# One moving part of 512 slots for the first products of the second mixture of experts

## The chip, the cores and the metric

The kernel runs on one core of a Trainium2 chip. The metric is device time in microseconds (us) of one execution, the median of several; lower is better. TensorE is called PE in the profile, VectorE DVE, ScalarE ACT, GpSimd POOL, and SyncE's DMA queue SP.

## What is computed

The reference chains linear attention, a dense two-layer network and a mixture of experts. The part that is changed is the last:

```python
for e in range(E):                      # 8 experts
    for k in range(2):                  # a token's first and second choice
        mask = top2[:, k] == e
        h = np.maximum(x[mask] @ w1[e], 0.0)        # [tokens, 512] @ [512, 1024]
        out[mask] += top2_w[mask, k, None] * (h @ w2[e])   # [tokens, 1024] @ [1024, 512]
```

There are 2304 tokens of 512 values; each goes to two of eight experts, so an expert has about 576 of them.

## The kernel before

Each expert has room for 640 slots (`CAP`), five blocks of 128 (`NB`); the first four are the early ones (`EARLY` = 512). All arithmetic of the experts is in pairs of fp32r numbers: a value is kept as a high part and the rest, and `mm3` (L170) makes one product out of three matmuls: high by high (L173), high by low (L174) and low by high (L175).

For an expert `e` these steps exist. `gather(e, j)` (L862) fetches a block of 128 token rows with indirect DMAs on POOL: one DMA of whole rows for experts 0 and 1 (L871), four DMAs of quarter rows for experts 2 to 7 (L866). `gtrans(e, j)` (L875) turns the block (on PE for experts 0 and 1, on DVE for the others) and splits it into `xgT[e]`, contraction on the partitions. `load_w1`, `load_w2` fetch the weights through SP, and `split_w1`, `split_w2` split them on ACT and DVE. `h2_step(e, f)` (L888) makes one of eight blocks of 128 hidden units: the stationary operand is a 128 by 128 block of `s1`, the moving one `xgT[e]` over the slots, the contraction has four parts, so with `mm3` there are twelve matmuls for each moving part. The result is then taken out of PSUM on ACT (relu, high part, L902) and DVE (low part, L903) into `hT`. `y2_step(e, j)` (L908) makes the second product for one block of slots, 24 matmuls of 512 columns with `hT` stationary, scales it on ACT, and adds it to the output with an indirect DMA on POOL (L917).

The moving part of `h2_step` is at most 512 columns, so 640 slots go in two: 384 and 256 (`HALVES`), both in one PSUM tile of two banks from the pool `py`, which has two such tiles. Step f+2 therefore needs step f to be out of PSUM. For expert 0 the first 512 slots are made early, during the last routing work (`PARTS[:1]`), and the last 128 later (`PARTS[1:]`, eight steps of twelve matmuls of 128 columns), between the second products of its blocks 2 and 3.

The order of all instructions is written out by hand (`tc.manual_schedule`): each engine runs its instructions in the order of the program, and semaphores are set from the tiles' dependencies. In the loop over experts from 1 on (L1095), the gathers and `load_w1` of the next expert come first in program order, then eight `h2_step`s of this expert with `split_w2` after every second, then `load_w2` of the next expert, then five `y2_step`s with the next expert's `split_w1` and `gtrans` between them.

Of the kernel before, what the change touches and what calls it, by code (L numbers as in the profile page):

```python
# [7 lines left out]
F32 = mybir.dt.float32  # L8
F32R = mybir.dt.float32r
# [3 lines left out]
AF = mybir.ActivationFunctionType  # L13
ALU = mybir.AluOpType
# [24 lines left out]
def attn_moe_moe2_kernel(  # L39
# [14 lines left out]
    nc = tc.nc  # L54
    B, H, S, D = q.shape
    NT = B * S
    DM = H * D
    DFF = w_in.shape[1]
    E, _, F2 = w1.shape
    P = 128  # L60
# [3 lines left out]
    NPR = DM // P  # L64
# [3 lines left out]
    NF2 = F2 // P  # L68
    CAP = 640
    NB = CAP // P  # L70
    EB = 4
    EARLY = EB * P
    PARTS = [(0, EARLY), (EARLY, CAP - EARLY)]
    HALVES = [(0, 384), (384, CAP - 384)]
    NE = 2
    NOB = (NT - CAP + P - 1) // P
    LSTRIDE = CAP + NOB * P
# [24 lines left out]
    ident = cst.tile([P, P], F32, name="ident")  # L102
# [32 lines left out]
    py = work.enter_context(tc.tile_pool(name="py", bufs=2, space=PSUM))  # L135
    pa = work.enter_context(tc.tile_pool(name="pa", bufs=2, space=PSUM))
# [5 lines left out]
    def SS(shape, dt, name):  # L142
        return sp.tile(shape, dt, tag="S", name=name)

    def XX(shape, dt, name):
        return xp.tile(shape, dt, tag="X", name=name)

    def HH(shape, dt, name):
        return hp.tile(shape, dt, tag="H", name=name)
# [4 lines left out]
    def TT(shape, dt, name):  # L154
        return tp.tile(shape, dt, tag="T", name=name)

    def MM(shape, name):
        return pm.tile(shape, F32, tag="M", name=name)

    def split_lo(lo, src, hi, eng=None):  # L160
        (eng or nc.vector).tensor_tensor(out=lo, in0=src, in1=hi.bitcast(F32), op=ALU.subtract)  # L161

    def split(alloc, src, shape, name, eng=None):
        hi = alloc(shape, F32R, name + "h")
        lo = alloc(shape, F32R, name + "l")
        nc.scalar.copy(hi, src)
        split_lo(lo, src, hi, eng)
        return hi, lo

    def mm3(out_ap, stat, mov, ssl, msl, start, stop):  # L170
        sh, sl = stat
        mh, ml = mov
        nc.tensor.matmul(out_ap, sh[ssl], mh[msl], start=start, stop=False)  # L173
        nc.tensor.matmul(out_ap, sh[ssl], ml[msl], start=False, stop=False)  # L174
        nc.tensor.matmul(out_ap, sl[ssl], mh[msl], start=False, stop=stop)  # L175
# [8 lines left out]
    def quarters_transposed(t, name):  # L184
        u = TT([P, NPR, P], F32, name)
        nc.vector.transpose(out=u.rearrange("p c (g a) -> p g c a", a=Q), in_=t.rearrange("p g (c b) -> p g c b", b=Q))
        return u
# [626 lines left out]
    raw1, raw2, s1, s2, xg, xgT, hT = {}, {}, {}, {}, {}, {}, {}  # L814

    def load_w1(e, i):
        raw1[e, i] = (HH if e == 0 else SS)([P, F2], F32, f"w1_{e}_{i}")
        nc.sync.dma_start(out=raw1[e, i], in_=quads(w1[e], i) if e >= NE else w1[e, i * P:(i + 1) * P, :])

    def load_w2(e, i):  # L820
        raw2[e, i] = SS([P, 2, DM], F32, f"w2_{e}_{i}")
        nc.sync.dma_start(out=raw2[e, i], in_=w2[e, 2 * i * P:2 * (i + 1) * P, :].rearrange("(a p) c -> p a c", p=P))

    def split_w1(e, i):
        s1[e, i] = split(W, raw1[e, i], [P, F2], f"s1_{e}_{i}")

    def split_w2(e, i):
        s2[e, i] = split(W, raw2[e, i], [P, 2, DM], f"s2_{e}_{i}", nc.gpsimd if e == 0 and i < 2 else None)
# [46 lines left out]
    def gtrans(e, j):  # L875
        if j == 0:
            xgT[e] = (XX([P, NPR, CAP], F32R, f"xgh{e}"), XX([P, NPR, CAP], F32R, f"xgl{e}"))
        if e >= NE:
            t = quarters_transposed(xg[e, j], f"xgt{e}_{j}")
        else:  # L880
            t = MM([P, NPR, P], f"xgp{e}_{j}")
            for c in range(NPR):
                nc.tensor.transpose(t[:, c, :], xg[e, j][:, c * P:(c + 1) * P], ident)
        hi, lo = (u[:, :, j * P:(j + 1) * P] for u in xgT[e])
        nc.scalar.copy(hi, t)
        split_lo(lo, t, hi)

    def h2_step(e, f, parts=HALVES):  # L888
        if len(parts) == 2:
            ps = py.tile([P, 2, DM], F32, tag="Y", name=f"h2_{e}_{f}")  # L890
            banks = [ps[:, i, :] for i in range(2)]
        else:
            banks = [pa.tile([P, DM], F32, tag="A", name=f"h2_{e}_{f}_{parts[0][0]}")]
        for (a, n), bk in zip(parts, banks):
            for c in range(NPR):
                mm3(bk[:, :n], s1[e, c], xgT[e], (slice(None), slice(f * P, (f + 1) * P)),
                    (slice(None), c, slice(a, a + n)), c == 0, c == NPR - 1)
        if (e, f // 2) not in hT:
            hT[e, f // 2] = (HH([P, 2, CAP], F32R, f"hTh{e}_{f}"), HH([P, 2, CAP], F32R, f"hTl{e}_{f}"))
        for (a, n), bk in zip(parts, banks):  # L900
            hi, lo = (t[:, f % 2, a:a + n] for t in hT[e, f // 2])
            nc.scalar.activation(hi, bk[:, :n], AF.Relu)  # L902
            nc.vector.scalar_tensor_tensor(out=lo, in0=bk[:, :n], scalar=0.0, in1=hi.bitcast(F32),  # L903
                                           op0=ALU.max, op1=ALU.subtract)

    adds = {}

    def y2_step(e, j, between={}):  # L908
        ps = pa.tile([P, DM], F32, tag="A", name=f"y2_{e}_{j}")
        for f in range(NF2):  # L910
            mm3(ps, tuple(t[:, f % 2] for t in hT[e, f // 2]), s2[e, f // 2], (slice(None), slice(j * P, (j + 1) * P)), (slice(None), f % 2),
                f == 0, f == NF2 - 1)
            if f in between:
                between[f]()
        t = TT([P, DM], F32, f"y2s{e}_{j}")
        nc.scalar.activation(t, ps, AF.Copy, scale=lst[:, e, j, 1:2].bitcast(F32))  # L916
        i = nc.gpsimd.indirect_dma_start(out=out, out_offset=bass.IndirectOffsetOnAxis(ap=lst[:, e, j, 0:1], axis=0),  # L917
                                         in_=t, in_offset=None, compute_op=ALU.add)
        nc.gpsimd.memset(spacer, 0)


        for o in adds.get(e, []):
            tc.declare_no_dep(i.ins, o.ins, reason="a token has one slot of an expert")
        for o in adds.get(e - 1, []):
            tc.add_manual_dep(i.ins, o.ins.name, mybir.DependencyInfo(mybir.DependencyClass.Sync, mybir.DependencyReason.DATA),
                              reason="adds to the same rows")
        adds.setdefault(e, []).append(i)


    with tc.manual_schedule():  # L930
# [64 lines left out]
        for g in range(NG):  # L995
# [42 lines left out]
            for f in range(NF):  # L1038
                ps = h_step(g, f)
# [32 lines left out]
            load_w1(1, i)  # L1072
        rus = route_units(NG - 1)
        for f in range(NF2):
            h2_step(0, f, PARTS[:1])
            for x in PLAN["r5"].split():
                if int(x.split("@")[1]) == f:
                    rus[x.split("@")[0]]()
            if f % 2:
                split_w2(0, f // 2)  # L1080
# [8 lines left out]
        for j in range(EB, NB):  # L1089
            gather(0, j)  # L1090
            gather(1, j)
        y2_step(0, 0)
        y2_step(0, 1)
        y2_step(0, 2, {4: lambda: gtrans(0, 4)})
        for e in range(E):  # L1095
            nx = e + 1 < E
            if nx and e:
                for j in range(NB):
                    gather(e + 1, j)
                for i in range(NPR):  # L1100
                    load_w1(e + 1, i)
            for f in range(NF2):
                h2_step(e, f, HALVES if e else PARTS[1:])
                if e and f % 2 == 0:
                    split_w2(e, f // 2)
                if e == 0 and f % 2:
                    gtrans(1, f // 2)
            if nx:
                for i in range(NF2 // 2):
                    load_w2(e + 1, i)  # L1110
            for j in range(NB):
                if e == 0 and j < EB - 1:
                    continue
                if nx:
                    if e:
                        if j < NPR:
                            split_w1(e + 1, j)
                        gtrans(e + 1, j)
                    elif j == EB - 1:
                        for i in range(NPR):  # L1120
                            split_w1(1, i)
                    else:
                        gtrans(1, j)
                y2_step(e, j)
    work.close()


    with ExitStack() as oc:
# [5 lines left out]
        with tc.If(most > CAP):  # L1134
            with tc.For_i(0, E, 1) as e:
# [7 lines left out]
                for m in range(NOB):  # L1143
# [3 lines left out]
                    pt = op.tile([P, NPR, P], F32, name="opt")  # L1147
# [12 lines left out]
                    for f in range(NF2):  # L1160
# [4 lines left out]
                        out=out, out_offset=bass.IndirectOffsetOnAxis(ap=ol[:, m, 0:1], axis=0),  # L1165
# [31 lines left out]
```

## Time and profile before

| | |
|---|---|
| median of three runs | 1051.83 us (1051.07 to 1052.28) |
| the profiled execution | 1058.36 us |
| its span, first to last instruction | 1056.7 us |
| PE busy | 968.6 us, 92% |
| experts 1 to 7, first to last product | 572.77 to 1043.34 us |
| mean granted TensorE clock | 0.952 of full |

The page tells busy time for each engine and, in 40 slices, where it falls. "Idle before, releaser" is the time an engine sat idle ahead of an instruction and what ended it. "issue" means that nothing shown released it, "remote" that a semaphore came in whose sender isn't known. The times of matmuls overlap, so what one costs in a stream is read from start to start, not from its own length.

### The profile page before, as it was taken

How to read it: one execution, taken by the hardware profiler on the slowest of the kernel's cores; microseconds unless marked ns; L12 is line 12 of the kernel's file. 1: busy time of each engine (PE TensorE's matmuls, PEld its weight loads, DVE VectorE, ACT ScalarE, POOL GpSimd, SP SyncE). 2: the span in 40 equal slices, each digit the busy share in tenths (PEclk: the TensorE clock that was granted, in tenths of full speed). 3: DMA queues.
4: the chain of work that ended last, by engine and by line, in shares of the span. 5: the costliest groups of instructions: out<-in, count | busy, mean ns of one | idle time of the engine just before them, and what ended most of it. 6: DMA issues, size and time to landing. Idle time of an engine off the chain costs nothing.

```text
span 1056.7 us, 12905 instructions
## 1 busy us (share of the span) xinstructions
PE 968.6 (92%) x4897; PEld 818.0 (77%) x4897; DVE 553.7 (52%) x978; ACT 427.1 (40%) x688; POOL 293.9 (28%) x342
## 2 busy tenths in 40 slices
PE   7989799999999999999999599697996997969994
PEld 7457578888888888898789499686886886868993
DVE  7899947964795567568434143242432523325320
ACT  3756544634463445467424132232331422314320
POOL 4002100150024003106342515427145162361111
PEclk8999899999999999999999799899898998989998
DMA  7688508600800120030652335244252442522203
GB/s 208 199 234 210 68 1 190 209 2 18 177 17 1 46 55 1 1 120 22 239 137 70 120 85 125 70 117 113 71 120 80 113 127 62 126 92 61 31 11 41
DMA packets 107282, 100.08 MB, mean 95 GB/s; under 512 B 58320, under 2 KB 82896, under 8 KB 107216
## 3 DMA queue, kind: packets, MB, share of 16 engines
q1 hardware_dynamic: 95664, 78.17, 26.2%
q0 software_dynamic: 11552, 21.04, 10.6%
q8 instruction: 40, 0.66, 0.3%
q14 instruction: 26, 0.21, 0.1%
HBM read 78.46 MB, written 20.72 MB: 94 GB/s over the span
## 4 chain that ended last, share of the span: by engine, by line
PE 74%; DVE 9%; issue 6%; another core or an unknown queue 5%; ACT 4%; DMA 1%; POOL 0%; DVEq 0%; POOLq 0%; SPq 0%; ACTq 0%
PE y L174 12%; PE y L173 12%; PE y L175 12%; PE h L175 11%; PE h L173 11%; PE h L174 10%; PE xp L495 2%; DVE stage L566 2%; ACT hTh L902 1%; PE kvp L381 1%; DVE hTl L903 1%; DVE stage L565 1%; PE qTp L482 1%; DVE hs L613 1%
## 5 line engine op out<-in xcount | busy, mean ns | idle before, releaser
L903 DVE SCALAR_TENSOR_TENSOR hTl<-h,hTh 128x384 fp32r<-128x384 f32 (+3 forms) x128 | 62.8, 491 | 233.7 <-ACT hTh L902 168.3
L902 ACT ACTIVATE hTh<-h 128x384 fp32r<-128x384 f32 (+3 forms) x128 | 56.0, 438 | 228.4 <-PE h L175 83.2
L917 POOL DMA_INDIRECT out_dram<-y2s,lst x40 | 63.3, 1581 | 282.9 <-ACT y2s L916 282.6
L866 POOL DMA_INDIRECT xg<-x2d,lq x120 | 118.9, 991 | 35.9 <-issue 33.1
L613 DVE SCALAR_TENSOR_TENSOR hs<-hs 128x512 f32<-128x512 f32 (+1 forms) x80 | 55.2, 690 | 54.5 <-ACT hs L612 52.7
L173 PE MATMUL h<-xgh,s_0h 128*128 128x384 f32 (+3 forms) x128 | 43.9, 343 | 43.1 <-DVE hTl L903 25.0
L438 POOL TENSOR_TENSOR q<-q,qm 128x1024 f32<-128x1024 f32 (+1 forms) x10 | 18.2, 1818 | 209.3 <-DVE qm L437 132.0
L612 ACT COPY hs<-h 128x512 f32<-128x512 f32 (+1 forms) x80 | 43.3, 541 | 76.7 <-PE h L175 73.1
L916 ACT ACTIVATE y2s<-y,lst 128x512 f32<-128x512 f32 x40 | 27.6, 689 | 91.3 <-PE y L175 76.4
L799 POOL DMA_INDIRECT lstd<-rrow,rsi x36 | 43.3, 1201 | 67.5 <-DVE rsi L796 61.6
L173 PEld LDWEIGHTS h<-xgh,s_0h 128*128 128x128 f32 x128 | 25.7, 201 | 46.9 <-DVE hTl L903 27.8
L624 ACT CAST g<-hs 128x512 fp32r<-128x512 f32 (+1 forms) x72 | 41.3, 573 | 37.8 <-DVE hs L613 37.7
L161 DVE TENSOR_TENSOR g<-hs,g 128x512 fp32r<-128x512 f32 (+1 forms) x72 | 44.9, 624 | 0.5 <-ACT g L624 0.5
L175 PE MATMUL h<-xgh,s_3l 128*128 128x384 f32 (+3 forms) x128 | 41.2, 322 | 2.9 <-issue 2.6
L175 PE MATMUL h<-xgh,s_0l 128*128 128x384 f32 (+3 forms) x128 | 41.9, 327 | 1.9 <-issue 1.9
L173 PE MATMUL h<-xgh,s_1h 128*128 128x384 f32 (+3 forms) x128 | 41.8, 327 | 1.7 <-issue 1.5
L174 PE MATMUL h<-xgl,s_0h 128*128 128x384 f32 (+3 forms) x128 | 42.1, 329 | 1.3 <-issue 1.3
L174 PE MATMUL h<-xgl,s_2h 128*128 128x384 f32 (+3 forms) x128 | 41.6, 325 | 1.1 <-issue 1.1
L173 PE MATMUL h<-xgh,s_2h 128*128 128x384 f32 (+3 forms) x128 | 41.4, 323 | 1.3 <-issue 1.3
L175 PE MATMUL h<-xgh,s_1l 128*128 128x384 f32 (+3 forms) x128 | 41.3, 323 | 1.3 <-issue 1.3
L174 PE MATMUL h<-xgl,s_1h 128*128 128x384 f32 (+3 forms) x128 | 41.5, 324 | 0.9 <-issue 0.8
L175 PE MATMUL h<-xgh,s_2l 128*128 128x384 f32 (+3 forms) x128 | 41.5, 324 | 0.6 <-issue 0.6
(341 smaller groups left out, 2914.4 us busy)
## 6 DMA issues: line engine op xcount, KB each, us to landing
w<-in_moe_w_dram SPq DMA_DIRECT2D x64, 512.0 KB
stage<-in_moe_w_in_dram SPq DMA_DIRECT2D x16, 512.0 KB
stage<-in_moe_w_out_dram SPq DMA_DIRECT2D x16, 512.0 KB
out_dram<-zero SPq DMA_DIRECT2D x1, 4864.0 KB
x2d<-x2s SPq DMA_DIRECT2D x9, 512.0 KB
k<-in_k_dram SPq DMA_DIRECT2D x12, 256.0 KB
v<-in_v_dram SPq DMA_DIRECT2D x12, 256.0 KB
x2q<-x2d SPq DMA_DIRECT2D x24, 128.0 KB
```

The source lines that it names most:

```text
L161: (eng or nc.vector).tensor_tensor(out=lo, in0=src, in1=hi.bitcast(F32), op=ALU.subtract)
L173: nc.tensor.matmul(out_ap, sh[ssl], mh[msl], start=start, stop=False)
L174: nc.tensor.matmul(out_ap, sh[ssl], ml[msl], start=False, stop=False)
L175: nc.tensor.matmul(out_ap, sl[ssl], mh[msl], start=False, stop=stop)
L612: nc.scalar.copy(hs, ps)
L613: nc.vector.scalar_tensor_tensor(out=hs, in0=hs, scalar=0.01, in1=hs, op0=ALU.mult, op1=ALU.max)
L624: nc.scalar.copy(parts[0], hs)
L799: i = nc.gpsimd.indirect_dma_start(out=lstd, out_offset=bass.IndirectOffsetOnAxis(ap=si[:, kk, r:r + 1], axis=0), in_=row[:, kk, r, :], in ...
L866: nc.gpsimd.indirect_dma_start(out=t[:, g, :], out_offset=None, in_=x2d.rearrange("n (i c) -> (n i) c", c=P), in_offset=bass.IndirectOffse ...
L902: nc.scalar.activation(hi, bk[:, :n], AF.Relu)
L903: nc.vector.scalar_tensor_tensor(out=lo, in0=bk[:, :n], scalar=0.0, in1=hi.bitcast(F32), op0=ALU.max, op1=ALU.subtract)
L917: i = nc.gpsimd.indirect_dma_start(out=out, out_offset=bass.IndirectOffsetOnAxis(ap=lst[:, e, j, 0:1], axis=0), in_=t, in_offset=None, com ...
```

## The change

`h2_step` now moves 512 slots in one part, into half a tile of `py`: steps f and f+1 share a tile, so two tiles hold four steps. The last 128 slots are made by a new function, `h2_late`: there the 128 slots are the stationary operand and the hidden units move, twice 512 columns, twelve matmuls each. The result has slots on the partitions; it goes through relu into two tiles of `TT` (one on ACT, one on DVE), and `turn`, called later, transposes it on PE in eight blocks of 128 by 128 into two tiles of `MM`, and splits it from there into the last 128 columns of `hT`. `turn` is called in the first `y2_step` of an expert after its sixth of eight blocks (for expert 0 in its fourth `y2_step`). All experts are treated so, expert 0 too. For expert 0 the `gtrans` of expert 1 and its `split_w1` are placed anew among the `y2_step`s, since the eight late steps that they lay between are gone.

```diff
-    HALVES = [(0, 384), (384, CAP - 384)]
-    def h2_step(e, f, parts=HALVES):
...
+    def h2_step(e, f):
+        n = EARLY
+        if f % 2 == 0:
+            h2p[e] = py.tile([P, 2, DM], F32, tag="Y", name=f"h2_{e}_{f}")
+            hT[e, f // 2] = (HH([P, 2, CAP], F32R, f"hTh{e}_{f}"), HH([P, 2, CAP], F32R, f"hTl{e}_{f}"))
+        ps = h2p[e][:, f % 2, 0:n]
+        for c in range(NPR):
+            mm3(ps, s1[e, c], xgT[e], (slice(None), slice(f * P, (f + 1) * P)),
+                (slice(None), c, slice(0, n)), c == 0, c == NPR - 1)
+        hi, lo = (t[:, f % 2, 0:n] for t in hT[e, f // 2])
+        nc.scalar.activation(hi, ps, AF.Relu)
+        nc.vector.scalar_tensor_tensor(out=lo, in0=ps, scalar=0.0, in1=hi.bitcast(F32),
+                                       op0=ALU.max, op1=ALU.subtract)
+
+    def h2_late(e):
+        a = EARLY
+        ps = py.tile([P, 2, DM], F32, tag="Y", name=f"h2l{e}")
+        for i in range(2):
+            for c in range(NPR):
+                mm3(ps[:, i, :], xgT[e], s1[e, c], (slice(None), c, slice(a, CAP)),
+                    (slice(None), slice(i * DM, (i + 1) * DM)), c == 0, c == NPR - 1)
+        t = [TT([P, DM], F32, f"h2l{e}_{i}") for i in range(2)]
+        nc.scalar.activation(t[0], ps[:, 0, :], AF.Relu)
+        nc.vector.tensor_scalar(out=t[1], in0=ps[:, 1, :], scalar1=0.0, scalar2=None, op0=ALU.max)
+
+        def turn():
+            for i in range(2):
+                pt = MM([P, NPR, P], f"h2lT{e}_{i}")
+                for c in range(NPR):
+                    nc.tensor.transpose(pt[:, c, :], t[i][:, c * P:(c + 1) * P], ident)
+                for j in range(NPR // 2):
+                    hi, lo = (u[:, :, a:CAP] for u in hT[e, i * NPR // 2 + j])
+                    nc.scalar.copy(hi, pt[:, 2 * j:2 * j + 2, :])
+                    split_lo(lo, pt[:, 2 * j:2 * j + 2, :], hi)
+        return turn
...
-        y2_step(0, 0)
-        y2_step(0, 1)
-        y2_step(0, 2, {4: lambda: gtrans(0, 4)})
-        for e in range(E):
+        y2_step(0, 0, {4: lambda: gtrans(1, 0)})
+        y2_step(0, 1, {4: lambda: gtrans(1, 1)})
+        y2_step(0, 2, {2: lambda: gtrans(0, 4), 5: lambda: gtrans(1, 2)})
+        turn = h2_late(0)
+        for i in range(NF2 // 2):
+            load_w2(1, i)
+        split_w1(1, 0)
+        split_w1(1, 1)
+        y2_step(0, 3, {5: turn})
+        split_w1(1, 2)
+        y2_step(0, 4, {1: lambda: gtrans(1, 3), 3: lambda: split_w1(1, 3), 5: lambda: gtrans(1, 4)})
+        for e in range(1, E):
...
             for f in range(NF2):
-                h2_step(e, f, HALVES if e else PARTS[1:])
-                if e and f % 2 == 0:
+                h2_step(e, f)
+                if f % 2 == 0:
                     split_w2(e, f // 2)
-                if e == 0 and f % 2:
-                    gtrans(1, f // 2)
+            turn = h2_late(e)
...
-                y2_step(e, j)
+                y2_step(e, j, {} if j else {5: turn})
```

## Rows read from the trace of the kernel before

**Rows 1.** The page, part 1: busy time, share of span, instructions.
```profile
PE 968.6 (92%) x4897; PEld 818.0 (77%) x4897; DVE 553.7 (52%) x978; ACT 427.1 (40%) x688; POOL 293.9 (28%) x342
```

**Rows 2.** First products by stretch (experts 1, 2, 6, 7): length, PE, PEld, DVE, ACT, clock, DMA.
```profile
572.77:618.64 45.87, 34.44 (x192) 32.45 (x191) 6.87 (x14) 6.05 (x14) 0.81 0.35 104
645.87:686.81 40.94, 31.73 (x192) 30.62 (x191) 6.87 (x14) 6.14 (x14) 0.87 0.32 86
...
919.57:960.60 41.03, 31.68 (x192) 30.23 (x191) 6.87 (x14) 6.14 (x14) 0.88 0.30 87
987.83:1015.95 28.12, 28.12 (x192) 28.08 (x191) 6.88 (x14) 6.14 (x14) 1.00 0.07 10
```

**Rows 3.** Timeline of ACT, experts 3 and 0: start, us, operation, idle before, releaser.
```profile
726.00 0.49 ACT L902 ACTIVATE hTh<-h 128x384 fp32r<-128x384 f32 x1 [3.22 <-PE h L175]
...
738.17 0.49 ACT L902 ACTIVATE hTh<-h 128x384 fp32r<-128x384 f32 x1 [9.73 <-issue]
...
746.03 0.49 ACT L902 ACTIVATE hTh<-h 128x384 fp32r<-128x384 f32 x1 [6.36 <-remote]
...
510.32 0.60 ACT L902 ACTIVATE hTh<-h 128x512 fp32r<-128x512 f32 x1 [2.23 <-PE h L175]
```

**Rows 4.** Timeline of PE, experts 3, 1 and 0.
```profile
724.47 0.28 PE L175 MATMUL h<-xgh,s_3l 128*128 128x256 f32 x1
...
727.99 0.28 PE L175 MATMUL h<-xgh,s_3l 128*128 128x256 f32 x1
...
733.17 0.28 PE L175 MATMUL h<-xgh,s_3l 128*128 128x256 f32 x1
740.18 0.69 PE L173 MATMUL h<-xgh,s_0h 128*128 128x384 f32 x1 [6.73 <-DVE hTl L903]
...
600.98 0.58 PE L173 MATMUL h<-xgh,s_1h 128*128 128x256 f32 x1 [1.02 <-issue]
602.38 0.37 PE L174 MATMUL h<-xgl,s_1h 128*128 128x256 f32 x1 [0.82 <-issue]
...
509.89 0.39 PE L175 MATMUL h<-xgh,s_3l 128*128 128x512 f32 x1
```

**Rows 5.** Timeline of POOL: gathers, first and last of 20, and of eight.
```profile
717.32 1.01 POOL L866 DMA_INDIRECT xg<-x2d,lq  x1 [0.19 <-issue]
...
742.07 0.94 POOL L866 DMA_INDIRECT xg<-x2d,lq  x1 [0.30 <-issue]
...
497.42 0.98 POOL L871 DMA_INDIRECT xg<-x2d,lst  x1 [4.05 <-PE y L175]
...
507.02 0.95 POOL L871 DMA_INDIRECT xg<-x2d,lst  x1 [0.31 <-issue]
```

**Rows 6.** Stretch in expert 3: length, PE, PEld, DVE, ACT, POOL, clock, DMA.
```profile
736.00:738.00 2.00, 0.00 (x0) 0.00 (x0) 0.00 (x0) 0.00 (x0) 1.70 (x2) 0.50 0.23 66
```

**Rows 7.** Timeline of PE: starts that give prices per matmul.
```profile
755.96 0.40 PE L173 MATMUL y<-s_0h,hTh 128*128 128x512 f32 x1
...
783.19 0.33 PE L173 MATMUL h<-xgh,s_0h 128*128 128x384 f32 x1
...
549.02 0.22 PE L173 MATMUL h<-xgh,s_0h 128*128 128x128 f32 x1
...
551.65 0.62 PE L883 MATMUL xgp<-ident,xg 128*128 128x128 f32 x4
552.03 0.31 PE L173 MATMUL h<-xgh,s_0h 128*128 128x128 f32 x1
...
561.30 0.47 PE L173 MATMUL y<-s_0h,hTh 128*128 128x512 f32 x1
```

**Rows 8.** Groups of DVE and ACT: evacuation of 512 columns.
```profile
L903 DVE SCALAR_TENSOR_TENSOR hTl<-h,hTh 128x512 fp32r<-128x512 f32 x8 | 5.5, 691 | 11.1 <-ACT hTh L902 10.8 <-issue 0.4
...
L902 ACT ACTIVATE hTh<-h 128x512 fp32r<-128x512 f32 x8 | 4.8, 598 | 11.3 <-PE h L175 9.2 <-PE tot L1082 2.1
```

**Rows 9.** A stretch of the dense network: length, PE, PEld, DVE, ACT, POOL, clock, DMA.
```profile
300.00:400.00 100.00, 100.00 (x487) 82.06 (x485) 64.87 (x117) 47.31 (x73) 17.09 (x20) 1.00 0.11 27
```

More of the change, by code (lines that the diff above doesn't have):

```diff
@@ L886, in gtrans @@
         split_lo(lo, t, hi)
-    def h2_step(e, f, parts=HALVES):
[L889 to L894, printed above, removed]
-            for c in range(NPR):
[L896 to L904, printed above, removed]
+    h2p = {}
@@ L1074, in attn_moe_moe2_kernel @@
         for f in range(NF2):
-            h2_step(0, f, PARTS[:1])
+            h2_step(0, f)
             for x in PLAN["r5"].split():
@@ L1091, in attn_moe_moe2_kernel @@
             gather(1, j)
-        y2_step(0, 0)
-        y2_step(0, 1)
-        y2_step(0, 2, {4: lambda: gtrans(0, 4)})
-        for e in range(E):
+        y2_step(0, 0, {4: lambda: gtrans(1, 0)})
[10 more added lines that the diff above has]
+        for e in range(1, E):
             nx = e + 1 < E
-            if nx and e:
+            if nx:
                 for j in range(NB):
@@ L1111, in attn_moe_moe2_kernel @@
             for j in range(NB):
-                if e == 0 and j < EB - 1:
-                    continue
                 if nx:
[L1115 to L1123, printed above, removed]
-                y2_step(e, j)
+                    if j < NPR:
+                        split_w1(e + 1, j)
+                    gtrans(e + 1, j)
+                y2_step(e, j, {} if j else {5: turn})
     work.close()
```

## The prediction

> **What bounds the kernel now.** I read the page first: PE is busy 92% of the span, no other engine over 52% [rows 1]. So PE's own work sets the time, and what it loses has to be found by stretch. The view by stretches, restricted to the first products, is the one that matters: the same 192 matmuls take 28.12 us for expert 7 and 45.87, 40.94 and 41.03 us for experts 1, 2 and 6 [rows 2] (six stretches of 40.9 to 45.9 us, experts 1 to 6, 251.7 us in all). Expert 7 is the one with no next expert to fetch. Against 6 x 28.12 = 168.7 us the six lose 83.0 us, the largest loss in the kernel.
>
> Where it goes is seen in expert 3, side by side on three engines. PE starts the last matmul of steps 2, 3 and 4 at 724.47, 727.99 and 733.17 [rows 4]. ACT, which is idle, begins to take these steps out at 726.00, 738.17 and 746.03 [rows 3]: 1.2, 9.9 and 12.6 us after each matmul's recorded end. [...] The late releases begin some 7 us after the first of 20 gathers of the next expert (717.32) and end 4 us after the last one's start (742.07) [rows 5]. Inside, PE stutters: in expert 1 it starts one matmul in 1.40 us (600.98, 602.38) with only "issue" ahead of it [rows 4]. I call this the jam: while gathers run, PE's results are handed over late and slowly. The trace doesn't say why.
>
> **The change, part by part.**
>
> *PE's plain work.* A stream of 512-column matmuls costs (783.19 - 755.96) / 120 = 0.227 us each [rows 7]. An expert from 1 on now has 8 x 12 + 2 x 12 = 120 of them: 27.23 us. Four transposes cost 552.03 - 551.65 = 0.38 us [rows 7], so the eight of `turn` cost 0.76 us. Together 27.99 against 28.12 [rows 2]: 0.13 us less, 0.9 us for seven experts. So columns are not saved: 640 before, 512 plus 128 after; only the count of matmuls falls, 192 to 120, and eight transposes come in. Expert 0's late steps take 561.30 - 549.02 = 12.28 us with four groups of `gtrans` in them [rows 7], so 12.28 - 4 x 0.38 = 10.76 us for 96 matmuls of 128 columns. After: 24 x 0.227 + 0.76 = 6.21. That is 4.6 us less. The moved `gtrans` are the same work elsewhere. Sum 5.5 us less.
>
> [...] My row gives 0.095 us for a transposition in a stream [rows 7]. [...]
>
> *ACT and DVE.* One pass of 512 columns is 0.60 and 0.69 us [rows 8] for each step, some 1.4 us after its release to the free bank, against two passes before. The late part adds one pass to each engine and four pairs of 256 columns. The whole is as much as before: 6.1 us on ACT, 6.9 on DVE in 28 us [rows 2], so PE hides it. `h2_late` itself covers the last step's exit (5.4 us against 1.4), and the late exit has six blocks of the first second product (4.1 us) until `turn`. If that cover were gone, it would cost up to 1.4 us at each of these places.
>
> *Queues.* SP: expert 1's weights are asked for at the same place; the weight splits that free their buffers come after, as before. POOL: no gather and no add is moved past another. `gtrans(0, 4)` comes two blocks earlier, but behind two other `gtrans`, 0.6 us earlier in all; I take nothing (bounds 0 to 1 us). `turn` puts four copies on ACT ahead of the scaling of the first second product; they wait for transposes that PE does before it, so they are done by then.
>
> *The jam.* Its price after the change shows in no row. From below: nothing remains, 83.0 us are won, since eight gathers back to back (497.42 to 507.02) [rows 5] ran beside 512-column matmuls, and the step right after them, whose last matmul ends at 509.89 + 0.39, is taken out at 510.32 [rows 3, 4]: not late after 10.5 us of gathers, where in expert 3 releases were late after 7. From above: nothing is won. Between them I count matmuls. From 726.00 to 738.17 to 746.03 the jam let 24 matmuls through in 12.2 and 7.9 us [rows 3], 2.4 a microsecond, while PE wanted 192 / 28.12 = 6.8. Now it wants 1 / 0.227 = 4.4, a step has 12, and four steps fit in PSUM instead of two. At 2.4 a step is released every 5 us. Take the jam to run, as in expert 3, from 10.5 to 32 us after the first matmul. Step 3 ends at 10.9 and is released near 12, steps 4 to 7 near 17, 22, 27 and 32. Step 6 needs the tile of 2 and 3, free at 13.4: PE doesn't wait. `h2_late` needs that of 4 and 5, free at 23.4, and PE comes at 21.8: 1.6 us. The first second product needs step 7, out of PSUM at 33.4, as its 19th matmul, for which PE comes at 23.4 + 5.45 + 4.1 = 33.0 at best: 0.4 us. [...] I take 3.5 us for each of six, 21 of 83 remaining, nearer to the lower end, since the counted rows lie there: 62 us won.
>
> **The sum.** 1058.36 - 5.5 - 62 = 990.9 us for the profiled execution (its span is 1.7 less). The median of the timed runs stood 6.5 us under it, so 984 us.
>
> **The rivals.**
>
> 1. *Forecast: the jam is counted in matmuls, and mostly goes.* Remaining 0 to 36 us: 963 to 999 us. For it: one matmul at a time passes with nothing else shown to wait for, and 192 become 120. Chance 0.50.
>
> 2. *Half of it stays.* If the jam passes columns, not matmuls, a step of 12 x 512 columns takes 0.8 of the 7680 columns of an old one, so 8 us at the 10 us that those took in the mean. Step 5 is then released near 29 us and free at 30.4, and `h2_late` stands 8.6 us. I let 6 to 11 us remain per expert: 999 to 1029 us. Against it stands only that the stutter is by single matmuls [rows 4]. Chance 0.18.
>
> 3. *All of it stays.* If each handing-over is late by itself, as the 9.9 and 12.6 us would also allow, step 3 is released near 23 us, PE stands from 16.4 (after steps 4 and 5) to 24.4, and then `h2_late` waits for step 5 until 33: again 12 to 14 us. Only the plain work is won: 1046 us (1040 to 1052). [...] Chance 0.20.
>
> 4. *Slower: `turn` holds PE.* If the second product waits for the whole tile of `hT` and not for its own columns, its seventh block must wait, right behind `turn`, for four pairs of passes of 256 columns on ACT and DVE: about half of 0.60 and 0.69 us each [rows 8], 4 x 0.6 + 0.4 = 2.8 us, for eight experts 22 us. It decides if the jam gives back less than 22 - 5.5 = 17 us; with rival 3's jam the time is 1046 + 22 = 1068 us. Against it: in the dense network a tail of 128 columns of the x tiles is written for the router while PE reads their head, and PE is busy 100.00 of 100 us [rows 9]. Chance 0.12.
>
> **How the numbers follow.** The likeliest is the first, 984 us, with 963 to 999 as its own range. To leave out no more than 2 in 10 the range takes in rivals 2 and 3 but not 4: 962 to 1048. A measurement of this kernel tells about 0.2% (2 us) from no change. Faster: 0.50 + 0.18 + 0.15 of rival 3 = 0.83; the same: 0.04 of rival 3; slower: 0.12 and the rest, 0.13.
>
> **What would show it.** In the view by stretches each expert's first products, with the late ones, should take about 27.3 us for expert 7 and 28 to 33 for experts 2 to 6. In ACT's timeline the relu passes should follow the last matmul of a step within a few us also while gathers run; gaps of 8 to 10 us there, and PE idle ahead of step 6, are rival 3. PE idle behind the transposes of `turn`, released by DVE, is rival 4. Expert 0's late part should shrink from 12.3 to 5.5 us. The forecast falls if the gathers themselves, and not the count of matmuls, set the end of the jam.

## The result, and the profile after

| | before | after |
|---|---|---|
| median | 1052.05 us (1051.07 to 1055.19) | 1026.74 us (1024.09 to 1028.26) |
| ratio, 95% interval | | 0.975 (0.972 to 0.978) |
| the profiled execution | 1058.36 us | 1025.86 us |
| its span | 1056.7 us | 1024.2 us |

The change made the kernel faster by 2.5%, where 6.5% was forecast: 25 us of 68. The time lies in the range, but that is not the whole finding. The experiments below show that the change adds 54 us of its own and that what it wins is there only on some occasions: where the jam is absent, the same change makes the same kernel 5.2% slower.

The page of after, its lines for engine busy time, for the clock, and the group that holds the new cost; then one line of the view of waits (us in total, times, longest):

```profile
PE 947.4 (93%) x4385; PEld 759.2 (74%) x4385; DVE 553.8 (54%) x954; ACT 424.9 (41%) x664; POOL 305.7 (30%) x342
...
PEclk8999899999999999999999999999999999999998
...
L172 PE MATMUL h<-xgh,s_0h 128*128 128x512 f32 x64 | 28.5, 446 | 45.2 <-DVE hTl L901 42.4
...
PE h L172 <- DVE hTl L901: 42.4, 30, 2.0
```

The granted clock is 1.00 from 574.94 to 1010 us, where before it fell to 0.50 [rows 6]. But PE now stands 30 times, 1.4 us each, ahead of the first matmul of a step, for DVE's pass on the result of another step.

The view by stretches for the first products of experts 1 and 2, columns as in [rows 2], the 24 matmuls of `h2_late` included in the length:

```profile
574.94:609.23 34.29, 23.12 (x96) 17.52 (x95) 5.53 (x8) 4.78 (x8) 1.00 0.51 148
637.33:671.41 34.08, 23.15 (x96) 17.52 (x95) 5.53 (x8) 4.78 (x8) 1.00 0.40 117
```

All seven experts take 34.0 to 34.3 us, expert 7 too, which has no gathers beside it. So both halves of the old pattern are gone: no 41 to 46 us beside gathers, but also no 28 us without them [rows 2]. The timelines of PE, ACT and DVE in expert 2 show why, steps 0, 1 and 2:

```profile
637.33 0.39 PE L172 MATMUL h<-xgh,s_0h 128*128 128x512 f32 x1
...
639.83 0.39 PE L174 MATMUL h<-xgh,s_3l 128*128 128x512 f32 x1
641.63 0.50 PE L172 MATMUL h<-xgh,s_0h 128*128 128x512 f32 x1 [1.41 <-DVE hTl L901]
...
644.26 0.39 PE L174 MATMUL h<-xgh,s_3l 128*128 128x512 f32 x1
644.49 0.39 PE L172 MATMUL h<-xgh,s_0h 128*128 128x512 f32 x1
...
640.25 0.60 ACT L900 ACTIVATE hTh<-h 128x512 fp32r<-128x512 f32 x1 [1.98 <-PE h L174]
...
644.69 0.60 ACT L900 ACTIVATE hTh<-h 128x512 fp32r<-128x512 f32 x1 [2.90 <-PE h L174]
...
640.88 0.69 DVE L901 SCALAR_TENSOR_TENSOR hTl<-h,hTh 128x512 fp32r<-128x512 f32 x1 [6.82 <-ACT hTh L900]
```

Step 0 ends on PE at 640.22, ACT takes it from 640.25, DVE from 640.88 to 641.57, and only then, at 641.63, does PE begin step 1. Step 1 writes the other bank, but of the same tile. Step 2, in the other tile, follows step 1 without a gap (644.26, 644.49). A pair of steps costs 644.49 - 637.33 = 7.16 us, where 24 matmuls at 0.227 us [rows 7] are 5.45. That is 1.71 us for each pair, four pairs in eight experts: 54.7 us. The jam is gone as well. Gathers run from 640.42 to 667, and the relu pass of this expert's last step, nearly 26 us after the first gather, begins 0.04 us after the recorded end of the matmul that it waits for:

```profile
640.42 1.00 POOL L865 DMA_INDIRECT xg<-x2d,lq  x1 [0.19 <-PE h L174]
...
666.90 0.94 POOL L865 DMA_INDIRECT xg<-x2d,lq  x1 [0.31 <-issue]
...
665.74 0.39 PE L174 MATMUL h<-xgh,s_3l 128*128 128x512 f32 x1
...
666.17 0.60 ACT L900 ACTIVATE hTh<-h 128x512 fp32r<-128x512 f32 x1 [2.90 <-PE h L174]
```

No relu pass of experts 1 to 7 is more than 0.1 us late.

The account: 83 us of jam won, 54.7 lost to the new wait, the forecast 5.5 of plain work: 33.8, or 31 with the 2.8 us of plain work that are measured below. The two profiled executions stand 32.5 us apart.

### The profile page after: what moved, and what is told of

Read it like the earlier page. It is cut to its first block, busy times and chain, and to the rows that moved or that the text cites. A ratio compares the mean times of both kernels' runs of the same rounds, so it can differ in the third digit from the quotient of the medians.

```text
span 1024.2 us, 11883 instructions
## 1 busy us (share of the span) xinstructions
PE 947.4 (93%) x4385; PEld 759.2 (74%) x4385; DVE 553.8 (54%) x954; ACT 424.9 (41%) x664; POOL 305.7 (30%) x342
## 3 DMA queue, kind: packets, MB, share of 16 engines
q0 software_dynamic: 11552, 21.04, 11.0%
## 4 chain that ended last, share of the span: by engine, by line
PE 81%; DVE 7%; issue 5%; ACT 3%; DMA 1%; SPq 1%; POOL 0%; POOLq 0%; DVEq 0%; ACTq 0%
PE y L173 12%; PE y L172 12%; PE y L174 12%; PE h L172 11%; PE h L174 10%; PE h L173 10%; DVE hTl L901 3%; ACT hTh L900 2%; PE xp L494 2%; PE h2l L172 1%; PE h2l L174 1%; PE h2l L173 1%; PE h L598 1%; PE kvp L380 1%; PE y L633 1%
## 5 line engine op out<-in xcount | busy, mean ns | idle before, releaser
L901 DVE SCALAR_TENSOR_TENSOR hTl<-h,hTh 128x512 fp32r<-128x512 f32 x64 | 44.2, 691 | 168.1 <-ACT hTh L900 135.3
L900 ACT ACTIVATE hTh<-h 128x512 fp32r<-128x512 f32 x64 | 38.2, 597 | 157.9 <-PE h L174 145.6
L172 PE MATMUL h<-xgh,s_0h 128*128 128x512 f32 x64 | 28.5, 446 | 45.2 <-DVE hTl L901 42.4
L938 ACT ACTIVATE y2s<-y,lst 128x512 f32<-128x512 f32 x40 | 27.6, 690 | 69.1 <-PE y L174 55.7
L172 PE MATMUL y<-s_3h,hTh 128*128 128x512 f32 x80 | 32.1, 401 | 0.0
L172 PE MATMUL y<-s_2h,hTh 128*128 128x512 f32 x80 | 31.3, 391 | 0.0
L172 PE MATMUL y<-s_1h,hTh 128*128 128x512 f32 x80 | 31.3, 391 | 0.0
L172 PE MATMUL y<-s_0h,hTh 128*128 128x512 f32 x80 | 31.2, 390 | 0.0
L174 PE MATMUL y<-s_3h,hTl 128*128 128x512 f32 x80 | 31.2, 390 | 0.0
L174 PE MATMUL y<-s_2h,hTl 128*128 128x512 f32 x80 | 31.2, 390 | 0.0
L173 PE MATMUL y<-s_3l,hTh 128*128 128x512 f32 x80 | 31.2, 390 | 0.0
```

The costliest lines, as they stand in the source:

```text
L900: nc.scalar.activation(hi, ps, AF.Relu)
L901: nc.vector.scalar_tensor_tensor(out=lo, in0=ps, scalar=0.0, in1=hi.bitcast(F32), op0=ALU.max, op1=ALU.subtract)
```

## Experiments on the new wait

**Pairs.** The theory: PE waits because the second step of a tile follows the readers of the first. So both steps of a pair are made first, and both taken out after.

```diff
+        if f % 2 == 0:
+            return
+        for i in range(2):
+            ps = h2p[e][:, i, 0:n]
+            hi, lo = (t[:, i, 0:n] for t in hT[e, f // 2])
...
```

> The changed kernel with one edit: the two steps that share a PSUM tile make all their products first, and both are taken out after the second. Theory (the 30 waits of odd steps for the exit of the even step in the same tile are the whole new loss, and no late release comes back when PE runs without them): the eight steps of an expert take 21.9 us instead of 28.6, so 7 x 6.7 + 6.6 for expert 0, 53 us less than the changed kernel's 1027: about 974 us, with ACT's relu passes within 0.1 us of the pair's last matmul. Rival (at 4.4 matmuls a microsecond the late releases come back, only the pauses had kept them away): 21 to 83 us of the old loss return, 995 to 1050 us, with relu passes several us late while gathers run and a clock that falls to half.

Measured 1007.68 us (1005.46 to 1011.72), 0.957 of before (0.951 to 0.963). The timeline of PE has steps 2.72 us apart, 12 x 0.227, with no wait between them:

```profile
646.22 0.39 PE L172 MATMUL h<-xgh,s_0h 128*128 128x512 f32 x1
...
648.94 0.39 PE L172 MATMUL h<-xgh,s_0h 128*128 128x512 f32 x1
```

So the wait is gone, but only 19 of its 54 us came back. The stretches of experts 2, 4 and 7 (no tile filter here: POOL's column stands before the clock), and ACT's timeline at the end of expert 2's steps, with PE's last matmul of step 7, what follows it, and the last of the 20 gathers:

```profile
635.34:668.72 33.38, 29.23 (x122) 23.49 (x120) 9.74 (x11) 9.17 (x13) 21.33 (x22) 0.95 0.41 119
...
762.72:789.92 27.20, 27.20 (x122) 22.52 (x120) 10.43 (x12) 9.22 (x13) 20.62 (x20) 1.00 0.49 140
938.27:965.47 27.20, 27.20 (x121) 22.53 (x120) 10.43 (x12) 9.22 (x13) 1.68 (x2) 1.00 0.08 10
```

```profile
656.87 0.39 PE L174 MATMUL h<-xgh,s_3l 128*128 128x512 f32 x1
660.28 0.79 PE L172 MATMUL h2l<-s_0h,xgh 128*128 128x512 f32 x1 [3.02 <-issue]
...
662.93 0.94 POOL L865 DMA_INDIRECT xg<-x2d,lq  x1 [0.30 <-issue]
...
657.55 0.60 ACT L904 ACTIVATE hTh<-h 128x512 fp32r<-128x512 f32 x1 [8.24 <-PE h L174]
...
666.82 0.60 ACT L904 ACTIVATE hTh<-h 128x512 fp32r<-128x512 f32 x1 [6.38 <-remote]
```

The jam is back: the last pair's products end at 657.26 and their first pass begins at 666.82, 9.6 us late, and PE stands for "issue" meanwhile. In four experts (1, 2, 3 and 6) the first products lose 6 to 11 us. In two, 4 and 5, they lose nothing: passes are late there too, but PE waits for one only at the transposes of `turn`, 1.2 and 0.9 us. The rival of this run's expectation held: with the wait gone, the jam comes back.

**Banks.** The same question from the other side: the order of after, but `py` has four tiles of one bank, so each step has a tile of its own.

```diff
-    py = work.enter_context(tc.tile_pool(name="py", bufs=2, space=PSUM))
+    py = work.enter_context(tc.tile_pool(name="py", bufs=4, space=PSUM))
...
-        ps = h2p[e][:, f % 2, 0:n]
+        ps = py.tile([P, DM], F32, tag="Y", name=f"h2_{e}_{f}")
```

> The changed kernel with the pool of two PSUM tiles of two banks made into four tiles of one bank, one for each step, and nothing else moved: each step is taken out at once. Theory that the wait goes by the tile: it is gone here too, 974 us as with the pairs, to within 3 us. Rival (the wait is for the exit itself, whatever the tile): 1027 us as the changed kernel.

Measured 1008.41 us (1003.53 to 1012.34), 0.957 (0.951 to 0.964), the same as pairs; first products of 27.2 us in three experts and 35.2 to 35.6 in four. So the wait goes by the tile, not by the bank: the same order with as many banks has none when the tiles are apart.

## Experiments on what makes the jam

**No gathers.** The kernel before, with the gathers of experts 2 to 7 replaced by a constant.

```diff
-            for g in range(NQ):
-                nc.gpsimd.indirect_dma_start(out=t[:, g, :], ...
+            nc.gpsimd.memset(t, 0.5)
```

> The kernel before, with the gathers of experts 2 to 7 left out: each block of rows is filled with a constant on POOL instead. Theory (the late releases come from the gathers in flight): no relu pass is late, experts 1 to 6 take 28.1 us for their first products as expert 7 does, 83 us less: about 969 us. Rival (they come from the weight loads or from the steps' own exit): 1045 to 1052 us, the first products still 41 us.

Measured 972.98 us. Expert 2's first products, which took 40.94 us [rows 2]:

```profile
626.36:654.48 28.12, 28.12 (x193) 28.12 (x192) 11.39 (x18) 10.57 (x19) 3.99 (x7) 1.00 0.26 80
```

All seven take 28.12 or 28.13 us, and the run is 1053.96 - 972.98 = 81 us shorter than before beside it. Without the gathers there is no jam, and the 83 us are its cost.

**Pairs without gathers.** The same edit in pairs.

> The changed kernel with the pairs edit, and with the gathers of experts 2 to 7 left out (a constant is written on POOL instead). Theory (what the pairs kernel still loses is late releases beside gathers, 34 us): 974 us, every expert's first products with the late ones 27.4 us, no relu pass late, full clock from 130 us to the last 10. Rival (the pairs themselves cost that time): about 1008 us.

Measured 971.54 us, all first products 27.20 us. So what pairs lacked, 1008 - 972 = 36 us, goes with the gathers too.

**Pairs with whole rows.** Fewer gather DMAs for the same bytes: `NE` = 7 makes the gathers of experts 2 to 6 fetch whole rows, 5 DMAs for an expert in place of 20; PE transposes their blocks in place of DVE, and the rows of their `w1` are read in another order.

```diff
-    NE = 2
+    NE = 7
```

> The changed kernel with the pairs edit, and experts 2 to 6 gathered as experts 0 and 1 are: one DMA of whole rows for a block instead of four of quarter rows, the same bytes, and transposed on PE (5 x 0.38 us for each of five experts, 9.5 us more on PE). Their gathers take 6.3 us of POOL instead of 25. Theory (late releases set in after some time of gathers in flight, 7 us or more): they go for experts 1 to 5, which fetch 2 to 6, and stay for expert 6 (6 us): 1008 - 30 + 10 = about 988 us. Rival (they follow the bytes): 1008 + 10 = about 1018 us.

Measured 984.46 us (983.27 to 990.13), 0.935 (0.930 to 0.940). First products of 27.55 to 27.6 us beside five gathers (four transposes are among them), and 27.20 in expert 6, whose gathers are still 20. The bytes are not what jams: the queue that carries the gathers moves 21.04 MB in pairs and here. In expert 6 the passes are late, as beside 20 gathers elsewhere, but four steps fit in PSUM, as the prediction had it, and PE waits only 0.95 us, at `turn`. The last matmul of step 7 and the first pass of its pair, 4.0 us late:

```profile
880.62 0.39 PE L174 MATMUL h<-xgh,s_3l 128*128 128x512 f32 x1
...
884.98 0.60 ACT L904 ACTIVATE hTh<-h 128x512 fp32r<-128x512 f32 x1 [4.31 <-remote]
```

**One tile for all steps.** To see whether a slower PE escapes the jam by its pace alone: before, with one PSUM tile, so that each step waits for the exit of the last.

```diff
-            ps = py.tile([P, 2, DM], F32, tag="Y", name=f"h2_{e}_{f}")
+            if f == 0:
+                h2p[e] = py.tile([P, 2, DM], F32, tag="Y", name=f"h2_{e}_{f}")
+            ps = h2p[e]
```

> The kernel before, with all eight first-product steps of an expert from 1 on in one PSUM tile, so that each step waits for the exit of the one before: the matmuls are as many and as small as before, but PE makes a step in about 3.5 + 2.0 us, 4.4 matmuls a microsecond. Theory (what counts is the pace of matmuls beside the gathers): no late release; 44 us of first products for each of experts 1 to 7, clock at full, 1052 + 6 x 2 + 16 = about 1080 us. Rival (the gathers delay releases whatever the pace): every step beside the gathers waits some 8 to 10 us more, 4 of them in each of six experts, over 1200 us.

Measured 1193.17 us. The serial steps themselves cost more than I had put: expert 7 takes 50.45 us. But experts 1 to 6 take 59.2 to 62.0 us, so the jam is there as well. PE's last matmuls of two steps of expert 2, when ACT takes these steps out, and the last gather:

```profile
679.40 0.28 PE L175 MATMUL h<-xgh,s_3l 128*128 128x256 f32 x1
...
689.29 0.28 PE L175 MATMUL h<-xgh,s_3l 128*128 128x256 f32 x1
...
681.41 0.49 ACT L906 ACTIVATE hTh<-h 128x384 fp32r<-128x384 f32 x1 [7.58 <-remote]
...
694.14 0.49 ACT L906 ACTIVATE hTh<-h 128x384 fp32r<-128x384 f32 x1 [10.30 <-remote]
...
690.02 0.94 POOL L866 DMA_INDIRECT xg<-x2d,lq  x1 [0.30 <-issue]
```

They are 1.7 and 4.6 us late, at 24 matmuls in 50.45 / 8 = 6.3 us, 3.8 a microsecond. After makes 24 in 7.16 us, 3.4 a microsecond, and is never late. Both expectations missed the time. A pause after each step and a mean pace close to that of after did not keep the jam away here, so neither explains alone why after has none.

**512 and 128.** Before, with the parts cut at 512: still 192 matmuls and 640 columns.

```diff
-    HALVES = [(0, 384), (384, CAP - 384)]
+    HALVES = [(0, 512), (512, CAP - 512)]
```

> The kernel before, with its two moving parts made 512 and 128 columns instead of 384 and 256: the same 192 matmuls and 640 columns for a contraction part, and the first part as in the changed kernel. Alone a step takes 12 x 0.227 + 12 x 0.113 = 4.08 us, 4.5 us more for each of seven experts. Theory (the late releases count matmuls, so those of an expert lose what they lost before, 83 us in six): 1052 + 31, some 1075 to 1085 us. Rival (they count columns or only the pace of the first part, and the loss is that of the pairs kernel, 34 us): about 1035 us.

Measured 1054.74 us. Experts 5 and 7 (POOL's column stands before the clock):

```profile
842.76:883.60 40.84, 36.20 (x194) 31.04 (x192) 11.79 (x18) 10.45 (x19) 23.13 (x22) 0.92 0.37 100
979.13:1011.98 32.85, 32.85 (x194) 28.68 (x192) 11.79 (x18) 10.56 (x19) 1.68 (x2) 1.00 0.07 9
```

Without gathers the 192 matmuls take 32.85 us here against 28.12, yet beside gathers both kernels need about 41 us. That would fit a count of matmuls, which was my forecast's guess, but as well a jam that lasts as long as the gathers do, which begin at the same place in both. The loss, 45 us, lies between the two that were expected, so the run does not settle it.

## Experiments on where there is a jam at all

**Before with whole rows.** Is the change needed for whole rows to help? `NE` = 7 in the kernel before.

> The kernel before with one number changed: the gathers of experts 2 to 6 fetch whole rows (5 DMAs an expert instead of 20, the same bytes), and PE transposes their blocks; expert 7 keeps quarter rows. Theory: what makes PE's results late is the number of gather DMAs in flight, whatever the kernel's steps look like. Then five of the six jams (83.0 us in all) go to a few tenths of a us each, as in the kernel with pairs and whole rows (27.56 us against 27.2), the one behind expert 6's first products stays with about 12 us, and PE pays 25 blocks of four transposes at 0.38 us, 9.5 us. From the median of before, 1052: 1052 - 70 + 9.5 = 991 us, and first products of 28 to 29 us in experts 1 to 5. Rival: five DMAs are enough for a jam where PE makes 6.8 matmuls a microsecond and not 4.4, so that the change was needed first: first products of 33 us and more, 1020 us or more.

Measured 985.74 us, and the kernel before, run beside it on the same chip, took 975.8 us (974.38 to 977.78), not 1052. Neither expectation had this: here whole rows are 1.1% slower (ratio 1.011, 1.009 to 1.013), and expert 6 of this run, with 20 quarter-row gathers beside it, takes 28.12 us. There was no jam to be ended.

Runs made together share one chip. In five such groups before took 1047.7 to 1059.2 us, in three 973.2 to 978.1, and never both in one group. The next four runs were to tell what each kernel does in the second kind:

> The kernel before, unchanged, for its trace on a chip where it takes 976 us instead of 1054 (seen beside the last run). Theory: the jam is a property of some chips (or of what else runs beside them), and all of the 78 us between the two times is the jam: here first products of 28.1 us in all seven experts, no relu pass more than 2 us behind the matmul that it waits for, the gathers at the same places beside them. Rival: another part of the kernel is faster there, and the first products keep some of their 83 us. On a chip where the jam is there: 1050 to 1059 us and first products of 41 to 46 us.

> The changed kernel, unchanged, beside before on the same chip. Theory: the change adds a wait of 54 us and takes 5.5 us of plain work; the 83 us that it won are the jam's alone. Where before takes 976 us there is no jam to win, so the change is slower by 48 us there: 1024 us, ratio 1.05, with first products of 34.1 us. Rival: the wait of 54 us shrinks too where before is fast: under 1000 us. On a chip with the jam: 1024 to 1028 us, ratio 0.975.

> The changed kernel with both steps of a pair made before both are taken out (the wait removed), beside before on the same chip. Theory: without the wait and without the jam only the plain 5.5 us are left of the change: where before takes 976 us, 970 to 972 us, first products of 27.2 us, as in the run of it without gathers (971.54). Rival: the loss of 36 us that it had beside gathers is its own: 1005 us. On a chip with the jam: 1005 to 1012 us.

> The pairs with whole rows for experts 2 to 6, beside before on the same chip. Theory: whole rows save the jam alone and cost PE 25 blocks of four transposes (9.5 us) with what goes with them: where before takes 976 us they lose that, 980 to 985 us, slower than before. Rival: whole rows are worth something of their own: under 972 us. On a chip with the jam: 984 us, ratio 0.935.

They fell in a group with the jam: before 1048.35 us here (first products 39.3 to 41.1 us in six experts), after 1027.0, 0.977 (0.972 to 0.981); pairs 998 to 1015 us, 0.952 (0.946 to 0.958, from the two shorter of its four runs); pairs with whole rows 987.3, 0.939 (0.935 to 0.944). They repeat the first results and say nothing of the other kind. Two runs then fell in a group without the jam:

> The kernel before with whole rows for experts 2 to 6 once more, for a chip on which before takes 1050 us. Theory there: the number of gather DMAs makes the jam, so five of six jams go: 985 us as on the chip without a jam, and about 12 us for expert 6's, 997 us, first products of 28.5 us in experts 1 to 5. Rival: five gathers are enough for a jam at 6.8 matmuls a microsecond: 1020 us or more. Where before takes 976 us: 986 us again.

> The changed kernel once more beside before. Where before takes 976 us, theory: slower, 1024 us, first products of 34.1 us (the wait of 54 us is the program's own, and there is no jam to win); rival: under 1000 us. Where before takes 1050 us: 1027 us.

Before 975.65 us, with whole rows 985.51 (ratio 1.010), after 1026.0 us: **1.052 of before (1.048 to 1.055), slower by 5.2%**, where 1024 was expected. After takes the same time with and without the jam, as its rows there show, experts 2 and 7 and the wait:

```profile
637.74:671.83 34.09, 23.16 (x96) 17.52 (x95) 5.53 (x8) 4.78 (x8) 1.00 0.41 116
948.70:982.77 34.07, 23.15 (x96) 17.52 (x95) 5.53 (x8) 4.78 (x8) 1.00 0.06 9
...
PE h L172 <- DVE hTl L901: 45.2, 32, 2.0
```

Then one more group with the jam:

> The kernel before with whole rows for experts 2 to 6. Where before takes 1050 us, theory: the number of gather DMAs makes the jam, five of six go: 997 us, first products of 28.5 us in experts 1 to 5. Rival: five gathers are enough for a jam at 6.8 matmuls a microsecond: 1020 us or more. Where before takes 976 us: 986 us, as the two times before.

> The changed kernel with pairs (the wait removed). Where before takes 976 us, theory: the wait of 54 us is all that made the change slower there, so 1026 - 54 = 972 us and first products of 27.2 us, faster than before by 0.4%. Rival: something else of the change costs there as well: over 980 us. Where before takes 1050 us: 1000 to 1015 us again.

Before 1052.6 us; before with whole rows 996.99 us, 0.948 (0.946 to 0.950), where 997 was expected; pairs 1001.04, 0.953 (0.945 to 0.961). The stretches of before with whole rows, experts 5 (five gathers beside it) and 6 (twenty):

```profile
804.52:833.00 28.48, 28.29 (x192) 28.08 (x191) 6.86 (x14) 6.28 (x15) 1.00 0.40 111
862.28:903.68 41.40, 31.61 (x192) 31.06 (x191) 6.86 (x14) 6.13 (x14) 0.88 0.31 79
```

So fewer gather DMAs end the jam without any of the change: one number changed in the old kernel wins 56 us here, twice what the change does. The five are also over sooner, 813.08 - 807.61 = 5.5 us from the first start to the last where twenty take 25 [rows 5]; this run does not part their number from the time that they run. Last, a group without the jam:

> The changed kernel with pairs (the wait removed). Where before takes 976 us, theory: the wait of 54 us is all that made the change slower there, so 1026 - 54 = 972 us and first products of 27.2 us, faster than before by 0.4%. Rival: something else of the change costs there as well: over 980 us. Where before takes 1050 us: 998 to 1015 us again.

> The kernel before, unchanged, for its trace. Where it takes 976 us, theory: no jam, first products of 28.1 us in all seven experts beside the same 20 gathers, no relu pass more than 2 us behind its matmul. Rival: the first products keep part of their 83 us. Where it takes 1050 us: 39 to 46 us of first products in six experts, as before.

Pairs 972.64 us (969.92 to 974.31), 0.997 of before (0.995 to 0.9985), where 972 was expected; before 974.56. Without the wait the change is no longer slower. Experts 2 and 6 of before there, and its gathers beside expert 2, first and last of 20:

```profile
626.77:654.89 28.12, 28.12 (x192) 28.08 (x191) 6.88 (x14) 6.14 (x14) 1.00 0.42 120
848.18:876.31 28.13, 28.13 (x192) 28.08 (x191) 6.87 (x14) 6.14 (x14) 1.00 0.45 121
```

```profile
629.85 1.01 POOL L866 DMA_INDIRECT xg<-x2d,lq  x1 [0.19 <-issue]
...
656.40 0.94 POOL L866 DMA_INDIRECT xg<-x2d,lq  x1 [0.30 <-issue]
```

The same program with the same gathers, over 26.5 us, much as in [rows 5], and no relu pass is more than 0.1 us late (ACT's come 3.5 us apart throughout).

## Why the prediction was wrong

| | forecast | with the jam | without |
|---|---|---|---|
| jam won | 62 of 83 us | 83 (after), 83 - 36 = 47 (pairs) | none to win |
| new wait | 0 us | 54 us | 54 us |
| plain work | 5.5 us won | | 2.8 won (pairs, 975.4 to 972.64) |
| after | 984 us | 1026.7 us | 1026.0 us |

**The step that failed** is the one in the part on the jam: "a step has 12, and four steps fit in PSUM instead of two ... PE doesn't wait", and the like sentence on ACT and DVE, that a pass goes "to the free bank" and "PE hides it". Four steps fit in the banks, but in this program two steps of one tile don't overlap: the second waits until the first has been read out. I priced the exits of ACT and DVE as hidden and gave 1.4 us as the price of one without its cover; it is 1.7 us, 32 times. I gave this wait no chance of its own, though the diff says that steps f and f+1 share a tile, and no row of before shows PE writing one half of a PSUM tile while the other is read. That should have been bounded from both sides: 0 to 32 x 1.4 = 45 us.

**Rival 4** had the mechanism and the wrong place. It let PE wait for a whole tile of `hT`, in SBUF. There it doesn't: PE goes from the eight transposes of `turn` straight on, as its timeline in after shows.

```profile
675.49 1.04 PE L921 MATMUL h2lT<-ident,h2l 128*128 128x128 f32 x8
676.29 0.48 PE L172 MATMUL y<-s_3h,hTh 128*128 128x512 f32 x1
```

The stretch from which I argued [rows 9] is about parts of SBUF tiles, and here they overlap as it says; of PSUM tiles it showed nothing. Its point from which it decides, 17 us of jam to win, holds for the real wait with other numbers: 54 less some 3 us must be won from the jam, which is so in one kind of group only.

**The jam, term by term.** That gathers cause it: right where it occurs (no gathers, 973 us). That a kernel with 120 matmuls keeps some 21 us of it, bounds 0 to 36: pairs, the kernel that I had in mind, keep 36, the upper end; it was mis-sized by 15 us. Of its 3.5 us for an expert 2 are counted, 1.6 and 0.4; the other 1.5 were an estimate that no run shows, and what the runs showed is 36 / 6 = 6 us in pairs and none in after. The lower bound stood on gathers of whole rows (L871 in [rows 5]), which make no jam in the old kernel either (28.48 us beside five of them), so it said nothing of quarter rows. After keeps none: two edits that take the wait out bring the jam back, so the wait kept it away; by what of its pauses is not shown. So the 62 us were won and more, but by luck: by a wait that the forecast did not have and that cost 54.

That "the gathers themselves, and not the count of matmuls, set the end of the jam" I named as what would make the forecast fall, and the rows say that they do. The last late pass begins 746.03 - 742.07 = 3.96 us after the start of the last gather in before [rows 3, 5], 666.82 - 662.93 = 3.89 in pairs and 694.14 - 690.02 = 4.12 with one tile for all steps; in the six experts of before it is 3.8 to 4.5, in the four of pairs that lose time 3.7 to 4.1. The prediction had read this 4 us in one expert and counted matmuls all the same. How many results pass while the jam lasts, and by what, stays open.

**Plain work.** The prices held: 120 matmuls in 27.20 us (27.23 forecast, pairs), eight transposes in 0.80 us from start to start (0.76). One transposition by itself is longer than that price: in the view of this tile in after, least, median and most in ns,

```profile
L921 PE MATMUL h2lT<-ident,h2l x64: 270/272/276, 566.3 to 987.1; 128*128 128x128 f32 x64
```

and 273 ns, the median, for those of `gtrans` in before. In a stream they overlap and cost 0.80 / 8 = 0.1 us each. The sum was too large all the same, 5.5 us against 2.8. From expert 0's first step to expert 1's, before without the jam takes 571.42 - 505.99 = 65.43 us and pairs 571.48 - 509.22 = 62.26, so 3.2 us are won and not 4.6; a later expert wins 55.35 - 55.31 = 0.04 us, not 0.13. Part of the first is pairs' own: its early steps take 25.76 us against 24.79.

**Queues and `h2_late`.** No delay showed there: gathers start at the same place, and expert 0's late steps take 5.5 us, as forecast.

**What I took for granted** was that before's three times speak for the kernel everywhere. They don't; the base of the whole prediction, 83 us of jam, is absent in three groups of eight. Nothing that I read in the one trace of before told me that.

## What to carry to other kernels

Where semaphores follow the tiles, as here, two halves of one PSUM tile are not a double buffer (1.71 us of wait for each pair of steps): give each accumulation a tile of its own, or make all products of a tile before any is read (no such wait in banks and in pairs), and in a diff look for tiles that came to be shared. When the largest loss in a profile is "issue" and late releases, undo its cause by itself (here the gathers, by one number) before reshaping the work around it. Run the unchanged kernel on several occasions and chips before a gain is believed: here the same change was 2.5% faster or 5.2% slower by the group in which it ran.

The version to keep depends on that. Pairs beat both kernels in either kind of group (0.952 to 0.957, and 0.997, which is little); pairs with whole rows are the best with the jam (0.935 to 0.939) and were not run without it, where before loses 1.0% by whole rows.

## What the runs showed of the hardware

**PE can fill one bank of PSUM while another is read out.** In after PE begins step 2 of expert 2 at 644.49, and ACT reads step 1 out of another bank from 644.69 to 645.29. The wait, 1.71 us for each pair in one tile, is the program's own, from semaphores that are set by tiles; with a tile for each bank there is none, and the products of an expert take 27.2 us in the three experts of banks that lose nothing. After changes the bank with every step and has no overlap in half of its steps; the overlap came with tiles of their own.

**Where the jam is, the recording loses marks.** I had not expected that one program differs by 76 us between groups. In the view of DMA issues, the gathers' line of before without the jam, and then of before with it:

```profile
xg<-x2d,lq POOLq DMA_INDIRECT x120, 3.1
```

```profile
xg<-x2d,lq POOLq DMA_INDIRECT x120
```

The first gives the time to landing, 3.1 us; the second can't, since marks of landings are missing in the trace file. For POOL's DMAs before's file holds 1407 of 3296 such marks (16 for each of 206 DMAs) with the jam and 3287 without it. All traces are of one kind or the other: the fifteen from groups with the jam hold 43 to 82% of these marks, the five from groups without it over 99%. Both files of before have all 12905 instructions and 107282 DMA packets, so it is marks of semaphores that are lost. The jam does not cause the loss. Of the 384 marks of the DMAs that POOL issued in the first 470 us, before any gather, the fifteen hold 195 to 264 and the five all; and the loss is there in after and in the kernels without gathers, which have no late pass. So in these runs the jam comes only where both are: a group in which marks are lost, and gathers of quarter rows.

Two things follow for reading such a trace. "issue" and "remote" may mean only that a mark is lost: for ACT's pass at 738.17 [rows 3] PE's mark is not in the file. And where the mark is there, the pass is prompt: for the one at 746.03, 12.6 us late, PE's mark stands at 746.007. So this lateness lies in PE's handing over, and not in ACT.

Whether the lost marks and the late passes have one cause no run here shows, since every time here comes with a span and a clock, so from a recorded execution. Whether chip, neighbours or recording make the difference stays open. The record gives the same chip number, 13, to a group without the jam and to one with it, three and a half minutes later; if that is one chip, the chip alone does not decide. Open, too, is what in a gather DMA matters: its packets, its count or how long the gathers run.
